# Strassen's seven block products, in fp16, for the output projection of a SwiGLU block behind cosformer attention

## The chip, the cores and the metric

The kernel runs on one core of a Trainium2 chip. The metric is the device time of one execution, in microseconds (us). Most executions of one kernel agree within 0.3%. The kernel before takes 324.7 us (median). Each run also has a profile of one execution: its span (first to last instruction, some 2 us less than the time), the busy time of each engine, and the clock that was granted to TensorE (1.00 is full speed).

The engines have short names in the profile: PE is TensorE (matmuls), PEld its weight loads, DVE VectorE, ACT ScalarE, POOL GpSimd, SP SyncE, which here only issues transfers.

## The reference

```python
# q, k, v: (8, 8, 576, 64) float32.  cosformer attention, then a SwiGLU block
q_p, k_p = phi(q), phi(k)             # relu, times cos and sin of the position
kv  = einsum('bhsf,bhsd->bhfd', k_p, v);  z = k_p.sum(axis=2)
x   = (q_p @ kv) / (q_p . z + 1e-6)   # reshaped to 4608 tokens x 512
g   = x @ w_gate                      # 512 x 1536
out = ((g * sigmoid(g)) * (x @ w_val)) @ w_out      # 1536 x 512
```

## The kernel before

The 4608 tokens are taken in nine groups of 512. For each group TensorE computes gate and value in 12 chunks of 128 hidden columns, with 8 matmuls of 512 columns per chunk. ScalarE makes silu out of PSUM (the memory that matmuls write, here used in eight banks), and VectorE multiplies it with the value into the hidden tile `ht`. Then comes the output projection: four token tiles, each a sum of 12 matmuls of 512 columns in one PSUM bank.

```python
def ffn_mul(tg, fc, lo=0, hi=GH):
    ...
    nc.vector.tensor_tensor(out=hts[tg % 2][:, fc, r:r + n], in0=sg[:, 0:n], in1=ps[1], op=ALU.mult)

def ffn_out(t, f0=0, f1=None):            # one tile of 128 tokens
    ...
    for fc in range(f0, f1):
        nc.tensor.matmul(out=o_ps[t], lhsT=hts[tg % 2][:, fc, r:r + P], rhs=wo_sb[:, fc],
                         start=(fc == 0), stop=(fc == FC - 1))
    ...
    (nc.scalar.copy if t % 2 == 0 else nc.vector.tensor_copy)(out=ob, in_=ps)
    # then two stores of 64 tokens each, on SyncE's queue
```

Work for later groups (the attention of the next batches) is put into numbered slots between these steps: q products (relu on ScalarE, then a multiplication with a table on VectorE), v products, and the normalisation of x. PSUM banks are handed out by a small allocator. It takes the bank that was used longest ago, but for output sums it first looks for a bank whose neighbour is taken, to keep pairs whole for others:

```python
def take(n, hold=None):
    taken = {x for r in held.values() for x in r}
    free = [b for b in range(0, 8, n) if not any(b <= x < b + n for x in taken)]
    b0 = min(free, key=lambda b: (n == 1 and hold is not None and hold[0] == "o" and b ^ 1 not in taken,
                                  sorted(used[b:b + n], reverse=True)))
    ...
```

Of the kernel before, what the change touches and what calls it, by code (L numbers as in the profile page):

```python
# [18 lines left out]
def kernel(  # L19
# [25 lines left out]
    NTG = NH // GH  # L45

# [8 lines left out]
    obp = ctx.enter_context(tc.tile_pool(name="obp", bufs=4))  # L55
# [55 lines left out]
    wo_sb = consts.tile([P, FC, d_model], BF16)  # L111
    hts = [consts.tile([P, FC, T], BF16, name=f"ht_{i}") for i in range(2)]
    first = {"q": consts.tile([P, G, QCUT, D], FP32, name="first_q")}

    for nm, home in (("v", wo_sb), ("k", hts[1])):
        flat = home.rearrange("p a b -> p (a b)")[:, 0:2 * G * NC * D]
        first[nm] = flat.bitcast(FP32).rearrange("p (g c d) -> p g c d", g=G, c=NC)
# [15 lines left out]
    pos_t = consts.tile([P, NW, SH], FP32)  # L133
# [46 lines left out]
    tabq = consts.tile([P, 2, NW, SH], FP16)  # L180
# [162 lines left out]
    qr = [consts.tile([P, 2, J, 2, SH], BF16, name=f"qr_{i}") for i in range(2)]  # L343
    qwT = [consts.tile([P, 2, 2, J, 2, SH], BF16, name=f"qwT_{i}") for i in range(2)]
# [61 lines left out]
    def x_den(t, ps, ys=slice(0, 4)):  # L406
        if ys.start == 0:
            st["den", t] = smp.tile([P, H, 1], FP32, name="den")
        nc.vector.tensor_single_scalar(
            out=st["den", t].rearrange("p (e y) o -> p e y o", e=2)[:, :, ys],  # L410
            in_=ps[:, :, 0:2 * J * D1].rearrange("p e (y x) -> p e y x", x=D1)[:, :, ys, D:D1], scalar=1e-6, op=ALU.add)
# [48 lines left out]
    def x_norm(t):  # L460
        num = st.pop(("num", t)).rearrange("p j e (i x) -> p (j e i) x", i=2)
        den = smp.tile([P, H, 1], FP32, name="den")
        nc.vector.tensor_single_scalar(out=den, in_=num[:, :, D:D1], scalar=1e-6, op=ALU.add)
        rec = smp.tile([P, H, 1], FP32, name="rec")
        nc.vector.reciprocal(out=rec, in_=den)
        x = xp.tile([P, d_model], BF16, name="x")
        for j in range(J):
            hs = slice(4 * j, 4 * j + 4)
            nc.vector.tensor_tensor(
                out=x[:, 4 * j * D:(4 * j + 4) * D].rearrange("p (i e d) -> p e i d", i=2, e=2),  # L470
                in0=num[:, hs, 0:D].rearrange("p (e i) d -> p e i d", e=2),
                in1=rec[:, hs].rearrange("p (e i) o -> p e i o", e=2).to_broadcast([P, 2, 2, D]), op=ALU.mult,
            )
        st["x", t] = x
# [41 lines left out]
    def ffn_silu(tg, fc, lo=0, hi=GH):  # L516
        n = (hi - lo) * SH
        sg = st["s", tg, fc, lo] = sgp.tile([P, T], BF16, name="sg")
        nc.scalar.activation(out=sg[:, 0:n], in_=st["f", tg, fc, lo][0], func=AF.Silu)  # L519

    def ffn_mul(tg, fc, lo=0, hi=GH):
        n, r = (hi - lo) * SH, lo * SH
        ps = st.pop(("f", tg, fc, lo))
        nc.vector.tensor_tensor(out=hts[tg % 2][:, fc, r:r + n], in0=st.pop(("s", tg, fc, lo))[:, 0:n], in1=ps[1],  # L524
# [14 lines left out]
    o_ps = {}  # L539

    def ffn_out(t, f0=0, f1=None):
# [4 lines left out]
        tg, i = divmod(t, GH // 2)  # L546
        r = i * P
        for fc in range(f0, f1):
            nc.tensor.matmul(out=o_ps[t], lhsT=hts[tg % 2][:, fc, r:r + P], rhs=wo_sb[:, fc],  # L549
                             start=(fc == 0), stop=(fc == FC - 1))  # L550
# [4 lines left out]
        ob = obp.tile([P, d_model], FP32, name="ob")  # L555
        (nc.scalar.copy if t % 2 == 0 else nc.vector.tensor_copy)(out=ob, in_=ps)  # L556
        for e in range(2):
            idx = 2 * t + e
            parts = 2 if NH - 10 <= idx < NH - 4 else 1
            for i in range(parts):  # L560
                cols = slice(i * d_model // parts, (i + 1) * d_model // parts)
                nc.sync.dma_start(out=out_v[idx // NC, idx % NC][:, cols], in_=ob[e * SH:(e + 1) * SH, cols])

    def ffn_out_last(t):

        tg, i = divmod(t, GH // 2)
        r = i * P
        for lo, hi in ((0, 320), (320, d_model)):
            ps = take(1)[:, 0:hi - lo]
            for fc in range(FC):  # L570
                nc.tensor.matmul(out=ps, lhsT=hts[tg % 2][:, fc, r:r + P], rhs=wo_sb[:, fc, lo:hi],
                                 start=(fc == 0), stop=(fc == FC - 1))
            ob = obp.tile([P, d_model], FP32, name="ob")
            nc.scalar.copy(out=ob[:, 0:hi - lo], in_=ps)
            for e in range(2):
                idx = 2 * t + e
                (nc.scalar if e else nc.sync).dma_start(out=out_v[idx // NC, idx % NC][:, lo:hi],
                                                        in_=ob[e * SH:(e + 1) * SH, 0:hi - lo])
# [132 lines left out]
    at((0, 1), turn(4), load_2)  # L711
# [69 lines left out]
    for tg in range(1, NTG):  # L781
        s0 = SLOTS * tg
        for fc in range(FC):
            ffn_fc(tg, fc)
            slot(s0 + fc)
        for i in range(OUT):
            if tg == NTG - 1 and i == OUT - 1:
                ffn_out_last(tg * OUT + i)
            else:
                ffn_out(tg * OUT + i)  # L790
            slot(s0 + FC + i)
# [31 lines left out]
```

## Time and profile before

| | kernel before |
|---|---|
| time, median of 4 | 324.67 us |
| span of the profiled execution | 322.9 us |
| TensorE busy | 316.3 us, 98% |
| VectorE busy | 181.0 us, 56% |
| one group's projection, first start to next start | 10.36 us |
| after the last matmul | 4.3 us |

Busy time is an average over stages, so it says who might bound a kernel, not who does. The chain of work that ended last says it: here TensorE has 93% of it. Matmuls overlap in their printed durations, so their cost is read from the distance between starts. The prediction shows these lines. The 4.3 us at the end are an estimate: the last 24 matmuls start at 316.01, and at the 0.109 us of a 256-column matmul (256 is their mean width) they need 2.62 us, which leaves 4.28 up to 322.9.

### The profile page before, as it was taken

To read this page: it belongs to the slowest core of one execution; us is meant where nothing else is said; L and a number is where in the kernel's file an instruction comes from. 1 tells how busy PE (TensorE), PEld (TensorE's weight loads), DVE (VectorE), ACT (ScalarE), POOL (GpSimd) and SP (SyncE) were. 2 spreads that over 40 slices of the span, in tenths; PEclk is the share of its full clock that TensorE was granted. 3 is DMA by queue.
4 is the path that set the end of the run, shared out by engine and by line. 5 is a ranking of instruction groups with operands and counts; after the bars stand their busy time and mean duration, and the time that the engine had idled before them with its cause. 6 is when DMAs were issued, how large, how long until landed. Compare 5 with 4: busy or idle time off the path is not lost.

```text
span 322.9 us, 6033 instructions
## 1 busy us (share of the span) xinstructions
PE 316.3 (98%) x2374; PEld 159.2 (49%) x2384; DVE 181.0 (56%) x363; ACT 130.5 (40%) x239; POOL 35.1 (11%) x60
## 2 busy tenths in 40 slices
PE   8899999999999999999999999999999999999994
PEld 4596555455445444544454445444544444444443
DVE  7873876786448747564756555755573236324320
ACT  7553556652346245333533354335432132213311
POOL 6845002010102000200011000200000000000000
PEclk9999999999999999999999999999999999999999
DMA  7999998988995987699769968895912401240014
GB/s 272 213 200 197 205 195 133 220 106 116 183 192 78 191 150 130 79 177 173 122 92 168 163 119 115 124 194 112 134 34 51 103 11 35 54 92 19 0 26 105
DMA packets 74861, 41.02 MB, mean 127 GB/s; under 512 B 50001, under 2 KB 69969, under 8 KB 74833
## 3 DMA queue, kind: packets, MB, share of 16 engines
q1 hardware_dynamic: 52480, 22.95, 38.9%
q0 software_dynamic: 22192, 17.57, 37.0%
q8 instruction: 18, 0.29, 0.4%
q10 hardware_dynamic: 160, 0.13, 0.1%
q14 instruction: 11, 0.08, 0.1%
HBM read 37.75 MB, written 9.44 MB: 146 GB/s over the span
## 4 chain that ended last, share of the span: by engine, by line
PE 93%; DVE 3%; ACT 2%; DMA 1%; issue 0%; ACTq 0%
PE banks L513 58%; PE banks L549 28%; PE banks L285 3%; PE banks L399 2%; PE banks L444 1%; PE banks L381 1%; DMA out_dram<-ob 1%; DVE v L239 1%; DVE raw_k L220 1%; PE banks L485 0%; DVE qwT L369 0%; ACT L184 0%; ACT phit L333 0%; ACT kvd L297 0%; ACT tabq L181 0%
## 5 line engine op out<-in xcount | busy, mean ns | idle before, releaser
L524 DVE TENSOR_TENSOR ht<-sg,banks 128x512 bf16<-128x512 bf16 (+2 forms) x116 | 74.6, 649 | 68.6 <-PE banks L513 62.1
L513 PE MATMUL banks<-xT,wv_sb 128*128 128x512 bf16 (+2 forms) x464 | 111.3, 364 | 0.0
L513 PE MATMUL banks<-xT,wg_sb 128*128 128x512 bf16 (+2 forms) x464 | 111.3, 364 | 0.0
L519 ACT ACTIVATE sg<-banks 128x512 bf16<-128x512 f32 (+2 forms) x116 | 65.8, 568 | 111.7 <-PE banks L513 109.1
L549 PE MATMUL banks<-wo_sb,ht 128*128 128x512 bf16 x410 | 93.1, 379 | 0.5
L513 PEld LDWEIGHTS <-wv_sb 128*128 128x128 bf16 x464 | 44.8, 98 | 48.7
L513 PEld LDWEIGHTS <-wg_sb 128*128 128x128 bf16 x464 | 43.1, 98 | 42.8
L549 PEld LDWEIGHTS <-ht 128*128 128x128 bf16 x420 | 40.3, 98 | 45.7 <-issue 0.2
L556 ACT COPY ob<-banks 128x512 f32<-128x512 f32 x18 | 10.5, 585 | 54.0 <-PE banks L549 54.0
L235 DVE TENSOR_TENSOR r_q<-raw_q,tab 128x1152 bf16<-128x1152 bf16 x24 | 17.9, 754 | 20.7 <-ACT raw_q L218 20.7
L556 DVE COPY ob<-banks 128x512 f32<-128x512 f32 x17 | 11.7, 691 | 28.7 <-PE banks L549 28.0
L239 DVE TENSOR_TENSOR v<-raw_v,tab 128x1152 bf16<-128x1152 bf16 x31 | 22.7, 752 | 0.3 <-ACT raw_v L583 0.3
L421 DVE TENSOR_TENSOR x<-banks,rec 128x512 bf16<-128x512 f32 (+1 forms) x32 | 21.6, 674 | 1.3 <-PE banks L381 0.3
L218 ACT ACTIVATE raw_k<-raw_k 128x576 bf16<-128x576 bf16 (+1 forms) x25 | 17.0, 694 | 0.0
L218 ACT ACTIVATE raw_q<-raw_q 128x576 bf16<-128x576 bf16 x24 | 15.5, 679 | 0.0
L732 POOL COPY hold<-phit 1x2 bf16<-1x2 bf16 x5 | 0.9, 175 | 130.5 <-DMA phit<-r_q 130.5
L399 PEld LDWEIGHTS <-phit 128*128 128x128 bf16 (+1 forms) x240 | 10.0, 100 | 6.5 <-issue 1.3
L399 PE MATMUL banks<-kv,phit 128*128 128x65 bf16 (+1 forms) x240 | 11.6, 195 | 0.0
L152 PE MATMUL banks<-zeros 128*128 128x64 bf16 (+1 forms) x64 | 9.4, 309 | 1.0 <-DVE zeros L147 1.0
L308 DVE CAST kv<-banks 64x260 bf16<-64x260 f32 x12 | 5.1, 428 | 7.4 <-ACT kv L308 7.3
L285 PEld LDWEIGHTS <-raw_k 64*64 64x64 bf16 x504 | 7.6, 106 | 3.0 <-issue 2.1
L285 PE MATMUL banks<-v,raw_k 64*64 64x130 bf16 x504 | 8.8, 218 | 0.0
(84 smaller groups left out, 130.7 us busy)
## 6 DMA issues: line engine op xcount, KB each, us to landing
out_dram<-ob SPq DMA_DIRECT2D x64, 128.0 KB, 2.4
raw_k<-in_k_dram POOLq DMA_DIRECT2D x7, 576.0 KB, 9.4
raw_q<-in_q_dram POOLq DMA_DIRECT2D x6, 576.0 KB, 6.5
raw_v<-in_v_dram POOLq DMA_DIRECT2D x6, 576.0 KB, 12.7
wo_sb<-in_moe_w_out_dram POOLq DMA_DIRECT2D x3, 512.0 KB, 12.8
wg_sb<-in_moe_w_gate_dram POOLq DMA_DIRECT2D x5, 256.0 KB, 9.2
wv_sb<-in_moe_w_val_dram POOLq DMA_DIRECT2D x5, 256.0 KB, 9.9
wo_sb<-in_v_dram SPq DMA_DIRECT2D x2, 576.0 KB, 4.1
```

The costliest lines, as they stand in the source:

```text
L152: nc.tensor.matmul(out=ps, lhsT=zeros, rhs=zeros[:, 0:cols].unsqueeze(1).to_broadcast([P, 4, cols]), start=True, stop=True)
L218: nc.scalar.activation(out=out, in_=in_, func=AF.Relu)
L235: nc.vector.tensor_tensor(out=st[b, "q"][:, g], in0=o.unsqueeze(2).to_broadcast([P, NC, 2, D]), in1=tab, op=ALU.mult)
L239: nc.vector.tensor_tensor(out=v2s[b % 2][:, g, :, :, 0:D], in0=(first if b == 0 and g == 0 else {"v": raw_of(b, "v")})["v"][:, g].unsqueez ...
L285: nc.tensor.matmul(out=ps[i * D:(i + 1) * D, e, j * 2 * D1:(j + 1) * 2 * D1], lhsT=raws[b, "k"][es, g, c], rhs=v2s[b % 2][es, g, c, :, 0:D ...
L399: nc.tensor.matmul(out=ps[ms, e, g * D1:(g + 1) * D1], lhsT=phit[b][:, e, g, c:c + n].rearrange("p c s -> p (c s)"), rhs=kv2s[b % 2][:, e, ...
L421: nc.vector.tensor_tensor(out=st["x", t].rearrange("p (y e d) -> p e y d", e=2, d=D)[:, :, ys], in0=ps[:, :, 0:2 * J * D1].rearrange("p e ...
L513: nc.tensor.matmul(out=st["f", tg, fc, lo][i], lhsT=(wg_sb, wv_sb)[i][:, kc, fs], rhs=xT[tg][:, ts, kc], start=(kc == 0), stop=(kc == KC - 1))
L519: nc.scalar.activation(out=sg[:, 0:n], in_=st["f", tg, fc, lo][0], func=AF.Silu)
L524: nc.vector.tensor_tensor(out=hts[tg % 2][:, fc, r:r + n], in0=st.pop(("s", tg, fc, lo))[:, 0:n], in1=ps[1], op=ALU.mult)
L549: nc.tensor.matmul(out=o_ps[t], lhsT=hts[tg % 2][:, fc, r:r + P], rhs=wo_sb[:, fc], start=(fc == 0), stop=(fc == FC - 1))
L556: (nc.scalar.copy if t % 2 == 0 else nc.vector.tensor_copy)(out=ob, in_=ps)
```

## The change

Strassen's scheme multiplies two matrices of 2 x 2 blocks with seven block products in place of eight, at the price of additions of blocks. Here the blocks are token halves and halves of the hidden dimension on one side, and hidden and output halves on the other. The intent is to take an eighth off the projection's TensorE time in groups 1 to 8. VectorE makes the sums of hidden blocks (S1 to S4) and adds the products; GpSimd makes the sums of weight blocks (T1 to T4) once. The sums need more mantissa bits, so hidden values and output weights are fp16, with x scaled by 4096 to stay clear of the smallest values. The change also keeps one hidden tile where two alternated.

```diff
-    wo_sb = consts.tile([P, FC, d_model], BF16)
-    hts = [consts.tile([P, FC, T], BF16, name=f"ht_{i}") for i in range(2)]
+    wo_sb = consts.tile([P, FC, d_model], FP16)
+    ht = consts.tile([P, FC, T], FP16, name="ht")
+    wt_sb = consts.tile([P, 4, HC, HD], FP16, name="wt_sb")
...
+    def weight_sums():
+        for o, x, y in ((T1, bq[:, 0, 1], bq[:, 0, 0]), (T2, bq[:, 1, 1], T1), (T3, bq[:, 1, 1], bq[:, 0, 1]),
+                        (T4, bq[:, 1, 0], T2)):
+            nc.gpsimd.tensor_tensor(out=o, in0=x, in1=y, op=ALU.subtract)
...
+    def sums_behind(fc):
+        for n, lo, hi in {7: ((3, 0, 4),), 8: ((1, 0, 4),), 9: ((2, 0, 4),), 10: ((4, 0, 4), (3, 4, 6)),
+                          11: ((1, 4, 6), (2, 4, 6), (4, 4, 6))}.get(fc, ()):
+            token_sum(n, lo, hi)
...
+        a = home("a")
+        product(a, aq[:, 0, 0], bq[:, 0, 0], True)
+        nc.scalar.mul(out=C12, in_=a[0], mul=DOWN)
+        e = home("e")
+        product(e, S3, T3, True)
+        added(C22, e, C12)
+        free("e")
+        slot_of(0)
+        b = home("b", nb)
+        product(b, S2, T2, True)
+        added(C21, b, C22)
+        product(a, aq[:, 1, 0], bq[:, 1, 0], False)
+        nc.scalar.mul(out=C11, in_=a[0], mul=DOWN)
+        free("a")
...
+        product(b, S1, T1, False)
+        added(C22, b, C22)
...
+        c = home("c")
+        product(c, aq[:, 1, 1], T4, True)
+        added(C21, c, C21)
...
+        product(b, S4, bq[:, 1, 1], False)
+        added(C12, b, C12)
...
-    at((0, 1), turn(4), load_2)
+    at((0, 1), turn(4), load_2, weight_sums)
```

A "home" in the code is a PSUM bank. In what follows the "third product" is S2T2, the third in TensorE's order, and the "fifth" is S1T1.

More of the change, by code (lines that the diff above doesn't have):

```diff
@@ L45 @@
     NTG = NH // GH
+    UP = float(2 ** 12)
+    DOWN = 1.0 / UP
+    HC = FC // 2
+    HT = T // 2
+    HD = d_model // 2
     consts = ctx.enter_context(tc.tile_pool(name="consts", bufs=1))
@@ L54 @@
     sgp = ctx.enter_context(tc.tile_pool(name="sgp", bufs=5))
-    obp = ctx.enter_context(tc.tile_pool(name="obp", bufs=4))
+    obp = ctx.enter_context(tc.tile_pool(name="obp", bufs=2))
     psum = ctx.enter_context(tc.tile_pool(name="psum", bufs=1, space=bass.MemoryType.PSUM))
@@ L110, with lodge @@
     CUT = 7
-    wo_sb = consts.tile([P, FC, d_model], BF16)
-    hts = [consts.tile([P, FC, T], BF16, name=f"ht_{i}") for i in range(2)]
-    first = {"q": consts.tile([P, G, QCUT, D], FP32, name="first_q")}
-    for nm, home in (("v", wo_sb), ("k", hts[1])):
+    wo_sb = consts.tile([P, FC, d_model], FP16)
+    ht = consts.tile([P, FC, T], FP16, name="ht")
+    wt_sb = consts.tile([P, 4, HC, HD], FP16, name="wt_sb")
+    spare = wt_sb.rearrange("p a b c -> p (a b c)")
+    taken_up = [0]
+    def lodge(n, dt):
+        o = taken_up[0]
+        taken_up[0] += n * (2 if dt == FP32 else 1)
+        assert taken_up[0] <= 4 * HC * HD
+        part = spare[:, o:taken_up[0]]
+        return part if dt == FP16 else part.bitcast(dt)
+    first = {"q": lodge(G * QCUT * D, FP32).rearrange("p (g c d) -> p g c d", g=G, c=QCUT)}
+    for nm, home in (("v", wo_sb), ("k", ht)):
         flat = home.rearrange("p a b -> p (a b)")[:, 0:2 * G * NC * D]
@@ L132 @@
     nc.gpsimd.iota(pos, pattern=[[1, NC]], base=0, channel_multiplier=NC, allow_small_or_imprecise_dtypes=True)
-    pos_t = consts.tile([P, NW, SH], FP32)
+    pos_t = lodge(NW * SH, FP32).rearrange("p (c s) -> p c s", c=NW)
     nc.gpsimd.iota(pos_t, pattern=[[1, NW], [NC, SH]], base=0, channel_multiplier=0,
@@ L179 @@
     csk, cst = cs_all[:, 0], cs_all[:, 1]
-    tabq = consts.tile([P, 2, NW, SH], FP16)
+    tabq = lodge(2 * NW * SH, FP16).rearrange("p (w c s) -> p w c s", w=2, c=NW)
     nc.scalar.activation(out=tabq[:, 0], in_=pos_t, func=AF.Sin, scale=-rad, bias=half_pi)
@@ L342 @@
     qf = consts.tile([P, 2, J, 2, D], BF16)
-    qr = [consts.tile([P, 2, J, 2, SH], BF16, name=f"qr_{i}") for i in range(2)]
-    qwT = [consts.tile([P, 2, 2, J, 2, SH], BF16, name=f"qwT_{i}") for i in range(2)]
+    qr = [lodge(4 * J * SH, BF16).rearrange("p (e j c s) -> p e j c s", e=2, j=J, c=2) for i in range(2)]
+    qwT = [lodge(8 * J * SH, BF16).rearrange("p (w e j c s) -> p w e j c s", w=2, e=2, j=J, c=2) for i in range(2)]
     def cast_q(c, eng):
@@ L408, in x_den @@
             st["den", t] = smp.tile([P, H, 1], FP32, name="den")
-        nc.vector.tensor_single_scalar(
+        nc.vector.tensor_scalar(
             out=st["den", t].rearrange("p (e y) o -> p e y o", e=2)[:, :, ys],
-            in_=ps[:, :, 0:2 * J * D1].rearrange("p e (y x) -> p e y x", x=D1)[:, :, ys, D:D1], scalar=1e-6, op=ALU.add)
+            in0=ps[:, :, 0:2 * J * D1].rearrange("p e (y x) -> p e y x", x=D1)[:, :, ys, D:D1],
+            scalar1=1e-6, scalar2=DOWN, op0=ALU.add, op1=ALU.mult)
     def x_rec(t, ps, ys=slice(0, 4)):
@@ L462, in x_norm @@
         den = smp.tile([P, H, 1], FP32, name="den")
-        nc.vector.tensor_single_scalar(out=den, in_=num[:, :, D:D1], scalar=1e-6, op=ALU.add)
+        nc.vector.tensor_scalar(out=den, in0=num[:, :, D:D1], scalar1=1e-6, scalar2=DOWN,
+                                op0=ALU.add, op1=ALU.mult)
         rec = smp.tile([P, H, 1], FP32, name="rec")
@@ L518, in ffn_silu @@
         sg = st["s", tg, fc, lo] = sgp.tile([P, T], BF16, name="sg")
-        nc.scalar.activation(out=sg[:, 0:n], in_=st["f", tg, fc, lo][0], func=AF.Silu)
+        nc.scalar.activation(out=sg[:, 0:n], in_=st["f", tg, fc, lo][0], func=AF.Silu, scale=DOWN)
     def ffn_mul(tg, fc, lo=0, hi=GH):
@@ L523, in ffn_mul @@
         ps = st.pop(("f", tg, fc, lo))
-        nc.vector.tensor_tensor(out=hts[tg % 2][:, fc, r:r + n], in0=st.pop(("s", tg, fc, lo))[:, 0:n], in1=ps[1],
+        nc.vector.tensor_tensor(out=ht[:, fc, r:r + n], in0=st.pop(("s", tg, fc, lo))[:, 0:n], in1=ps[1],
                                 op=ALU.mult)
@@ L539, with ob_of, store @@
     o_ps = {}
+    obs = {}
+    def ob_of(t):
+        h, i = divmod(t, 2)
+        if h not in obs:
+            obs[h] = obp.tile([P, 2, d_model], FP32, name="ob")
+        return obs[h][:, i]
+    def store(t, cols=slice(0, d_model), queues=None):
+        for e in range(2):
+            idx = 2 * t + e
+            (queues or (nc.sync, nc.sync))[e].dma_start(out=out_v[idx // NC, idx % NC][:, cols],
+                                                        in_=ob_of(t)[e * SH:(e + 1) * SH, cols])
     def ffn_out(t, f0=0, f1=None):
@@ L545, in ffn_out @@
             o_ps[t] = take(1, ("o", t))
-        tg, i = divmod(t, GH // 2)
-        r = i * P
+        r = t % OUT * P
         for fc in range(f0, f1):
-            nc.tensor.matmul(out=o_ps[t], lhsT=hts[tg % 2][:, fc, r:r + P], rhs=wo_sb[:, fc],
+            nc.tensor.matmul(out=o_ps[t], lhsT=ht[:, fc, r:r + P], rhs=wo_sb[:, fc],
                              start=(fc == 0), stop=(fc == FC - 1))
@@ L554, in ffn_out @@
         give_back(("o", t))
-        ob = obp.tile([P, d_model], FP32, name="ob")
-        (nc.scalar.copy if t % 2 == 0 else nc.vector.tensor_copy)(out=ob, in_=ps)
-        for e in range(2):
-            idx = 2 * t + e
-            parts = 2 if NH - 10 <= idx < NH - 4 else 1
-            for i in range(parts):
-                cols = slice(i * d_model // parts, (i + 1) * d_model // parts)
-                nc.sync.dma_start(out=out_v[idx // NC, idx % NC][:, cols], in_=ob[e * SH:(e + 1) * SH, cols])
@@ L564, in ffn_out_last @@
-    def ffn_out_last(t):
-        tg, i = divmod(t, GH // 2)
-        r = i * P
-        for lo, hi in ((0, 320), (320, d_model)):
-            ps = take(1)[:, 0:hi - lo]
-            for fc in range(FC):
-                nc.tensor.matmul(out=ps, lhsT=hts[tg % 2][:, fc, r:r + P], rhs=wo_sb[:, fc, lo:hi],
-                                 start=(fc == 0), stop=(fc == FC - 1))
-            ob = obp.tile([P, d_model], FP32, name="ob")
-            nc.scalar.copy(out=ob[:, 0:hi - lo], in_=ps)
-            for e in range(2):
-                idx = 2 * t + e
-                (nc.scalar if e else nc.sync).dma_start(out=out_v[idx // NC, idx % NC][:, lo:hi],
-                                                        in_=ob[e * SH:(e + 1) * SH, 0:hi - lo])
+        if t % 2 == 0:
+            nc.scalar.mul(out=ob_of(t), in_=ps, mul=DOWN)
+        else:
+            nc.vector.tensor_single_scalar(out=ob_of(t), in_=ps, scalar=DOWN, op=ALU.mult)
@@ new lines, in ffn_out @@
+        store(t)
+    aq = ht.rearrange("p (i w) (h t) -> p w h i t", w=2, h=2)
+    bq = wo_sb.rearrange("p (i w) (h x) -> p w h i x", w=2, h=2)
+    sums = consts.tile([P, 3, HC, HT], FP16, name="sums")
+    S1, S2, S3, S4 = aq[:, 0, 1], sums[:, 0], sums[:, 1], sums[:, 2]
+    T1, T2, T3, T4 = (wt_sb[:, i] for i in range(4))
+    def weight_sums():
+        for o, x, y in ((T1, bq[:, 0, 1], bq[:, 0, 0]), (T2, bq[:, 1, 1], T1), (T3, bq[:, 1, 1], bq[:, 0, 1]),
+                        (T4, bq[:, 1, 0], T2)):
+            nc.gpsimd.tensor_tensor(out=o, in0=x, in1=y, op=ALU.subtract)
@@ new lines, in token_sum @@
+    def token_sum(n, lo, hi):
+        o, x, y, op = {
+            3: (S3, aq[:, 0, 0], aq[:, 0, 1], ALU.subtract),
+            1: (S1, aq[:, 0, 1], aq[:, 1, 1], ALU.add),
+            2: (S2, S1, aq[:, 0, 0], ALU.subtract),
+            4: (S4, aq[:, 1, 0], S2, ALU.subtract),
+        }[n]
+        nc.vector.tensor_tensor(out=o[:, lo:hi], in0=x[:, lo:hi], in1=y[:, lo:hi], op=op)
+    def sums_behind(fc):
+        for n, lo, hi in {7: ((3, 0, 4),), 8: ((1, 0, 4),), 9: ((2, 0, 4),), 10: ((4, 0, 4), (3, 4, 6)),
+                          11: ((1, 4, 6), (2, 4, 6), (4, 4, 6))}.get(fc, ()):
+            token_sum(n, lo, hi)
@@ new lines, in out_by_quarters, with home, free, at_of @@
+    def out_by_quarters(tg, slot_of):
+        last = tg == NTG - 1
+        t0 = tg * OUT
+        for t in (t0, t0 + 2):
+            ob_of(t)
+        C11, C12 = (obs[t0 // 2][:, :, x * HD:(x + 1) * HD] for x in range(2))
+        C21, C22 = (obs[t0 // 2 + 1][:, :, x * HD:(x + 1) * HD] for x in range(2))
+        def home(nm, parts=1):
+            return [take(1, ("o", tg, nm, i)).rearrange("p (t x) -> p t x", x=HD) for i in range(parts)]
+        def free(nm, parts=1):
+            for i in range(parts):
+                give_back(("o", tg, nm, i))
+        def at_of(x, i):
+            return x[i][:, 0] if len(x) == 2 else x[0][:, i]
+        def product(to, a, b, first):
+            for i in range(2):
+                for kc in range(HC):
+                    nc.tensor.matmul(out=at_of(to, i), lhsT=a[:, kc, i * P:(i + 1) * P], rhs=b[:, kc],
+                                     start=first and kc == 0 and (i == 0 or len(to) == 2),
+                                     stop=kc == HC - 1, skip_group_check=True)
+        def added(o, ps, x):
+            for i in range(len(ps)):
+                sl = slice(i, i + 1) if len(ps) == 2 else slice(0, 2)
+                nc.vector.scalar_tensor_tensor(out=o[:, sl], in0=ps[i][:, 0:1] if len(ps) == 2 else ps[i],
+                                               scalar=DOWN, in1=x[:, sl], op0=ALU.mult, op1=ALU.add)
+        nb = 2 if last else 1
+        a = home("a")
[12 more added lines that the diff above has]
+        free("a")
+        if last:
+            for t in (t0, t0 + 1):
+                store(t, slice(0, HD))
+        slot_of(1)
+        product(b, S1, T1, False)
+        added(C22, b, C22)
+        if last:
+            for t in (t0 + 2, t0 + 3):
+                store(t, slice(HD, d_model))
+        c = home("c")
+        product(c, aq[:, 1, 1], T4, True)
+        added(C21, c, C21)
+        free("c")
+        for t in (t0 + 2, t0 + 3):
+            store(t, slice(0, HD) if last else slice(0, d_model))
+        slot_of(2)
+        product(b, S4, bq[:, 1, 1], False)
+        added(C12, b, C12)
+        free("b", nb)
+        for t in (t0, t0 + 1):
+            store(t, slice(HD, d_model) if last else slice(0, d_model), (nc.sync, nc.scalar) if last else None)
+        slot_of(3)
@@ L784 @@
             ffn_fc(tg, fc)
+            sums_behind(fc)
             slot(s0 + fc)
-        for i in range(OUT):
-            if tg == NTG - 1 and i == OUT - 1:
-                ffn_out_last(tg * OUT + i)
-            else:
-                ffn_out(tg * OUT + i)
-            slot(s0 + FC + i)
+        out_by_quarters(tg, lambda i: slot(s0 + FC + i))
     assert not plan, sorted(plan)
```

## The prediction

> **What bounds the kernel now.** I read the page first: busy shares, then the chain that ended last. Then the chain's lines by shape, then single stretches of the timeline.
>
> ```profile
> PE 316.3 (98%) x2374; PEld 159.2 (49%) x2384; DVE 181.0 (56%) x363; ACT 130.5 (40%) x239; POOL 35.1 (11%) x60
> ...
> PE 93%; DVE 3%; ACT 2%; DMA 1%; issue 0%; ACTq 0%
> PE banks L513 58%; PE banks L549 28%; PE banks L285 3%; PE banks L399 2%; PE banks L444 1%; PE banks L381 1%; DMA out_dram<-ob 1%; DVE v L239 1%; DVE raw_k L220 1%; PE banks L485 0%; DVE qwT L369 0%; ACT L184 0%; ACT phit L333 0%; ACT kvd L297 0%; ACT tabq L181 0%
> ```
>
> TensorE is the bound: 93% of the chain, with the output projection (L549) at 28% of it. TensorE never waits long on another engine, and the granted clock is 1.000. So whatever shortens TensorE's stream shortens the kernel, as long as no other engine starts to hold it up. What a matmul costs must be read from starts, since the printed durations overlap:
>
> ```profile
> 21.27 0.60 PE L513 MATMUL banks<-xT,wg_sb 128*128 128x256 bf16 x4
> 21.71 0.60 PE L513 MATMUL banks<-xT,wv_sb 128*128 128x256 bf16 x4
> 22.14 0.60 PE L513 MATMUL banks<-xT,wg_sb 128*128 128x256 bf16 x4
> 22.58 0.60 PE L513 MATMUL banks<-xT,wv_sb 128*128 128x256 bf16 x4
> 23.02 2.35 PE L513 MATMUL banks<-xT,wg_sb 128*128 128x256 bf16 x20
> 25.20 1.04 PE L513 MATMUL banks<-xT,wv_sb 128*128 128x256 bf16 x8
> ...
> 111.03 10.52 PE L549 MATMUL banks<-wo_sb,ht 128*128 128x512 bf16 x47
> ...
> 121.39 1.03 PE L513 MATMUL banks<-xT,wg_sb 128*128 128x512 bf16 x4
> ```
>
> From 21.27 to 25.20 there are 36 matmuls of 256 columns, each with its own weights: 3.93/36 = 0.109 us. One group's projection is 48 matmuls of 512 columns (47 recorded), from 111.03 to 121.39: 10.36/48 = 0.216 us. A half-width matmul with its own weight load costs half. This is what decides whether Strassen's smaller blocks pay on TensorE at all.
>
> **What the Trainium skill says.** "TensorE: Matmul & The Clock Gate", section "Back-to-back issue gap", gives a warm gap of N/2.4 + 2.5 ns: 109 ns at 256 columns and 216 at 512. The trace agrees to the nanosecond. (The same section's figure of about 131 ns for sustained 512-column matmuls does not fit here.)
>
> "VectorE: DVE Perf Modes", section "What auto-detection actually checks", says that a two-tensor operation reaches two elements a cycle when all tensors are 16-bit with unit step. The trace agrees: L235, 16-bit from SBUF, has 1152 elements in 754 ns, while L421, which reads PSUM, needs 691 ns for 512. The new token sums are of the first kind.
>
> "SBUF — State Buffer", section "Who interferes with whom", says that VectorE and GpSimd share a port pair that one instruction takes for its whole length; a VectorE operation in a two-port mode, or one with two SBUF inputs against a GpSimd instruction that reads SBUF, waits. The first three microseconds show the two-port case:
>
> ```profile
> 1.11 0.59 DVE L170 COPY posk<-pos 64x9 f32<-64x9 f32 x1
> 1.72 0.17 DVE L171 TENSOR_SCALAR posk<-pos 64x9 f32<-64x9 f32 x1
> ...
> 2.12 0.42 DVE L173 TENSOR_SCALAR ang<-posk 128x18 f32<-128x18 f32 x1
> ...
> 0.94 0.59 POOL L134 IOTA pos_t<- 128x512 f32 x1
> ...
> 1.99 0.53 POOL L142 MEMSET kvd<- 128x520 f32 x1
> ```
>
> L170 handles nine elements and takes 0.59 us, ending just after GpSimd's work; L171, of the same size, takes 0.17. L173 ends with the memset. The two-input case is not in this trace.
>
> "GPSIMD Engine Reference", section "Elementwise — side-by-side cycle accounting", gives 4497 ns for a two-input operation of 2048 elements. This trace has no such operation; scaled to 1536 elements my estimate is 3.4 us.
>
> **The change part by part.**
> *TensorE.* Groups 1 to 8 (group 0 keeps the old form) each replace 48 matmuls of 512 columns by 7 products x 2 token halves x 6 = 84 of 256 columns: 84 x 0.109 = 9.18 us for 10.36. That is 1.18 us a group, 9.4 us over eight, all on the chain. It is less than the eighth that the idea promises only through the 2 ns floor per matmul. Fp16 streams as bf16 does, I assume.
>
> *VectorE.* Each group gains four token sums, each cut into 1024 and 512 elements. L235's 754 ns for 1152 elements at 0.52 ns leaves 0.15 us fixed, so they are 0.68 and 0.41 us: 4 x 1.09 = 4.4 us. It gains five additions out of PSUM of 512 elements: L455 takes 483 ns for 260, at 1.04 ns an element, so 0.75 us for 512, together 3.75. It loses two copies of 0.69. Net +6.7 us a group, 54 us over all: 181 becomes 235, 74% of the span. In a middle group (121.4 to 154.9) VectorE has 14.8 + 5.0 = 19.8 us busy and would get 26.5 in about 32.4: no bound on average, but close in places.
>
> *ScalarE.* Two evacuations a group before, two after: nothing.
>
> *Coupling in the output stage.* This is new. One bank collects S2T2, then S1T1 on top, then S4B22 on top, and VectorE must read it before each further product, with one other product (1.31 us) to hide that. I placed a middle group's VectorE work on the old timeline, group 3, with the projection starting at 144.42. The multiplication of chunk 11 ends near 145.2, the three tail sums at 146.5, the pending q product at 147.2, the normalisation of the next x (1.04) at 148.25, the addition of S3T3 at 148.9, a q product at 149.6, the addition of S2T2 at 150.3. TensorE wants the bank at 144.42 + 4 x 1.31 = 149.66, so it waits about 0.65 us. The next reuse (at 152.9 against a read done at 152.5) fits. Groups 1 to 5 have q products in this place, in group 1 with later sums; groups 6 to 8 do not, and there the read ends in time. I book 5 x 0.6 = 3.0 us.
>
> *Weight sums on GpSimd.* Four two-input operations, 4 x 3.4 = 13.6 us, once, queued behind the loads of batch 2. They must be there for group 1's projection near 78 us, which is easy. But they start at about 51.05, when group 0's last x is made:
>
> ```profile
> 50.30 0.75 POOL L102 DMA_DIRECT2D raw_v<-in_v_dram  x1
> ...
> 51.67 0.17 DVE L463 TENSOR_SCALAR den<-num 128x8 f32<-128x8 f32 x1
> 51.87 0.20 DVE L465 RECIPROCAL rec<-den 128x8 f32<-128x8 f32 x1
> ...
> 52.11 0.76 DVE L469 TENSOR_TENSOR x<-num,rec 128x256 bf16<-128x256 f32 x2
> ...
> 53.00 0.39 PE L485 MATMUL banks<-ident,x 128*128 128x128 bf16 x4
> ```
>
> L463 is SBUF to SBUF like L173, L469 has two SBUF inputs, and TensorE transposes the result at 53.00 with 0.1 us to spare. If the first weight sum holds the ports until 54.45, x comes at about 55.65 and TensorE loses 2.7 us. If the second gets in between L463 and L469, it comes at about 58.9 and TensorE loses 5.9, and might fall to a lower clock after such a pause. If the lock does not bite, nothing. I book 2.0 us as a mean.
>
> *Ends.* The start only moves where small tables lie. At the end a 256-column addition on VectorE (about 0.48 us) takes the place of a 192-column copy (0.32) before the last stores: +0.2 us.
>
> Sum: 324.7 - 9.4 + 3.0 + 2.0 + 0.2 = 320.5.
>
> **The rivals.**
> *The full gain.* VectorE is earlier than I think, and GpSimd disturbs nothing: 324.7 - 9.4 = 315.3. For it: TensorE's share of the chain, and the half-width rate, which is measured. Against it: the dense VectorE queue.
> *VectorE paces every output stage.* If the sums run at one element a cycle, they cost about 3.3 us a group more; chunks 7 to 11 take TensorE some 9.2 us, and VectorE would be late for S2 and for each bank read, by 1.5 to 2.5 us a group: 324 to 330. Against it: L235's rate on like operands.
> *GpSimd's sums cost most of the gain.* Three blocked operations in a row, 6 to 10 us and a lower clock after it: 324 to 330. For it: L170 and L173. Against it: it happens only once, and later VectorE work has some 4 us of slack behind TensorE's eight banks.
> *Weight loads no longer hide.* A load is 98 ns busy, and a 256-column matmul leaves 109. Were they to add, the change would lose tens of microseconds; the 36 matmuls above exclude it.
>
> **Range and chances.** The 9.4 us are firm to half a microsecond. The output stalls can be 0.5 to 6 us, the GpSimd block 0 to 6, rarely 10. Both small gives 316; both large 326. Faster by over 2% means below 318.2, which needs the two together under 2.9 us: 0.30. Slower than 331.2 needs a rival in full: 0.05. The rest, 0.65, is within 2%.
>
> **What would show it.** The 256-column matmuls should start 0.109 us apart, and an undisturbed output stage should last 9.2 us; if they start farther apart without any wait, the first step is wrong. TensorE should wait for VectorE's additions once in each of groups 1 to 5, 0.4 to 0.8 us, and hardly in 6 to 8. The token sums should take 0.68 and 0.41 us; about 1.2 and 0.7 would show one element a cycle. The weight sums should take 3 to 4 us each, and between 51 and 59 us the lines that were L463 and L469 should be stretched, with TensorE idle before the transposes; if they are not, the port step is wrong. A granted clock under 1.0 after 53 us would be the part that I did not price.

## The result

The changed kernel takes 347.27 us (345.22 to 349.61 in four runs) beside 324.67 before. The ratio is 1.0699, with a 95% interval of 1.0642 to 1.0756. Here and below a ratio is the mean time of one kernel's fast runs over that of the other's of the same rounds, so it isn't quite the ratio of the medians. The outputs are correct. This is 7% slower, where I predicted 1.3% faster.

The page of the changed kernel, first its busy times, then the clock granted to TensorE in 40 equal slices (tenths), then the chain that ended last:

```profile
PE 310.9 (91%) x2660; PEld 186.5 (54%) x2660; DVE 236.6 (69%) x455; ACT 130.2 (38%) x237; POOL 47.9 (14%) x64
...
PEclk9999997699999999999999999999999999999997
...
PE 65%; DVE 13%; DMA 10%; SPq 4%; issue 3%; ACT 2%; DVEq 0%; POOLq 0%; POOL 0%; ACTq 0%
```

TensorE's busy time fell by 5 us and its share of the chain from 93 to 65%: it waits now, mostly for VectorE. VectorE has 236.6 us, where I had predicted 235. In two slices, 51 to 69 us, the clock fell (in the last slice TensorE has almost nothing to do). Most of the chain's 10% of DMA lies in groups 3 and 4: there the chain is followed back from an addition on VectorE over a q product to the transfers that brought its operand. TensorE ran without gaps during these transfers, so they are not lost time.

Where the 20.4 us between the spans came from is told by the starts of the stages on TensorE in both timelines:

| stage | before | after | difference |
|---|---|---|---|
| to the first matmul of group 1 | 54.09 | 63.60 | +9.51 |
| chunks of group 1 | 23.32 | 24.45 | +1.13 |
| projections of groups 1 to 5 | 51.8 | 57.6 | +5.8 |
| projections of groups 6 to 8 | 31.1 | 30.7 | -0.4 |
| after the last matmul | 4.3 | 8.6 | +4.3 |
| all other stages | | | 0.0 |

The chunk stages of groups 2 to 8 are among these, so the single hidden tile cost nothing there.

Three places, then. The first is the end of group 0's projection. GpSimd's, VectorE's and TensorE's timelines of the changed kernel (start, duration, engine, line, operation, output and input):

```profile
51.88 3.10 POOL L602 TENSOR_TENSOR wt_sb<-wo_sb 128x1536 f16<-128x1536 f16 x1
55.06 3.08 POOL L602 TENSOR_TENSOR wt_sb<-wo_sb,wt_sb 128x1536 f16<-128x1536 f16 x1
58.10 3.26 POOL L602 TENSOR_TENSOR wt_sb<-wo_sb 128x1536 f16<-128x1536 f16 x1
...
51.56 3.46 DVE L480 TENSOR_SCALAR den<-num 128x8 f32<-128x8 f32 x1
55.05 0.20 DVE L483 RECIPROCAL rec<-den 128x8 f32<-128x8 f32 x1
55.29 6.35 DVE L487 TENSOR_TENSOR x<-num,rec 128x256 bf16<-128x256 f32 x2
...
58.48 0.40 PE L503 MATMUL banks<-ident,x 128*128 128x128 bf16 x2 [5.43 <-DVE x L487]
61.70 0.40 PE L503 MATMUL banks<-ident,x 128*128 128x128 bf16 x2 [2.83 <-DVE x L487]
...
63.60 1.91 PE L531 MATMUL banks<-xT,wg_sb 128*128 128x512 bf16 x4
```

The den operation (the denominator of x), 0.17 us before, took 3.46 and ended with the first weight sum. Each of the two halves of x then ended with the second and the third: 6.35 us for 0.76. TensorE stood for 8.3 us, and then ran at half clock: the four matmuls at 63.60 are 1.91 us long, where those before were 1.03.

The second place is each projection. Group 2 of the changed kernel, where the bracket gives the idle time before an instruction and what ended it, and the same product of group 8:

```profile
122.51 1.47 PE L640 MATMUL banks<-wo_sb,ht 128*128 128x256 f16 x12
123.82 1.47 PE L640 MATMUL banks<-wt_sb,sums 128*128 128x256 f16 x12
127.55 1.47 PE L640 MATMUL banks<-wt_sb,sums 128*128 128x256 f16 x12 [2.26 <-DVE ob L647]
128.86 1.47 PE L640 MATMUL banks<-wo_sb,ht 128*128 128x256 f16 x12
...
126.82 0.68 DVE L647 SCALAR_TENSOR_TENSOR ob<-banks,ob 128x512 f32<-128x512 f32 x1
...
328.15 1.47 PE L640 MATMUL banks<-wt_sb,sums 128*128 128x256 f16 x12 [0.84 <-DVE ob L647]
```

A product is 12 matmuls, and products start 1.31 us apart: 0.109 us each, as predicted. But the third product does not follow the second. It waits for the addition of S3T3 on VectorE, in all eight groups, even in group 8, where VectorE stood idle before it. Start to start beyond 1.31 us, the eight waits are 1.84, 2.42, 2.40, 1.95, 2.23, 1.00, 1.21 and 1.00: 14.05 us. Less the 9.4 us that seven products save, that leaves +4.65; the two rows of the table give +5.4, and the rest is smaller waits, above all 0.2 us before the seventh product in groups 1 to 5.

Why should S2T2 wait for the reading of S3T3? The two need no common data. I wrote the allocator's answers down while building the kernel: for group 3 it gives bank 2 to `a`, 3 to `e`, and 3 again to `b`. (A second build with the answers printed confirms this, and shows the bank of `e` again in `b` in all eight groups.) The program gives `e` back just before it asks for `b`, and the neighbour of `a`, which is the bank of `e`, is what the allocator looks for first.

The third place is the end, from SyncE's and ScalarE's queues:

```profile
333.38 1.47 PE L640 MATMUL banks<-wo_sb,sums 128*128 128x256 f16 x12
...
331.59 9.36 SPq L570 DMA_DIRECT2D out_dram<-ob  x14
334.74 1.38 ACTq L570 DMA_DIRECT2D out_dram<-ob  x2
```

Sixteen stores fall due within the last three or four microseconds, and 14 of them are issued one after another on one queue: 9.36/14 = 0.67 us each. The kernel before had twelve on that queue, and two on ScalarE's, spread over the projection of the last group.

### The profile page after: what moved, and what is told of

It is laid out like the page before. It is cut to its first block, busy times and chain, and to the rows that moved or that the text cites. A ratio compares the mean times of both kernels' runs of the same rounds, so it can differ in the third digit from the quotient of the medians.

```text
span 343.3 us, 6710 instructions
## 1 busy us (share of the span) xinstructions
PE 310.9 (91%) x2660; PEld 186.5 (54%) x2660; DVE 236.6 (69%) x455; ACT 130.2 (38%) x237; POOL 47.9 (14%) x64
## 4 chain that ended last, share of the span: by engine, by line
PE 65%; DVE 13%; DMA 10%; SPq 4%; issue 3%; ACT 2%; DVEq 0%; POOLq 0%; POOL 0%; ACTq 0%
PE banks L531 40%; PE banks L640 18%; DMA phit<-r_q 5%; DMA raw_q<-in_q_dram 4%; DVE x L487 2%; SPq L570 2%; SPq L274 2%; DVE ob L647 2%; PE banks L301 2%; DVE ht L542 2%; DVE sums L611 2%; PE banks L580 2%; DVE den L480 1%; PE banks L415 1%; DVE r_q L251 1%
## 5 line engine op out<-in xcount | busy, mean ns | idle before, releaser
L542 DVE TENSOR_TENSOR ht<-sg,banks 128x512 f16<-128x512 bf16 (+2 forms) x116 | 74.6, 648 | 53.0 <-PE banks L531 44.6
L647 DVE SCALAR_TENSOR_TENSOR ob<-banks,ob 128x512 f32<-128x512 f32 (+1 forms) x43 | 28.0, 652 | 19.5 <-PE banks L640 18.5
L640 PEld LDWEIGHTS <-ht 128*128 128x128 f16 x384 | 37.1, 98 | 4.5
L640 PEld LDWEIGHTS <-sums 128*128 128x128 f16 x288 | 28.1, 98 | 18.3 <-issue 15.2
L640 PE MATMUL banks<-wt_sb,sums 128*128 128x256 f16 x192 | 23.6, 272 | 12.7 <-DVE ob L647 12.7
L640 PE MATMUL banks<-wo_sb,ht 128*128 128x256 f16 x192 | 23.6, 273 | 0.0
L640 PE MATMUL banks<-wt_sb,ht 128*128 128x256 f16 x192 | 22.3, 273 | 0.0
L663 ACT ACTIVATE ob<-banks 128x512 f32<-128x512 f32 x8 | 4.8, 597 | 36.4 <-PE banks L640 36.4
L611 DVE TENSOR_TENSOR sums<-ht 128x1024 f16<-128x1024 f16 (+1 forms) x32 | 17.7, 553 | 0.3
L580 PE MATMUL banks<-wo_sb,ht 128*128 128x512 f16 x48 | 13.0, 400 | 0.0
```

Source lines behind the costliest of these rows:

```text
L542: nc.vector.tensor_tensor(out=ht[:, fc, r:r + n], in0=st.pop(("s", tg, fc, lo))[:, 0:n], in1=ps[1], op=ALU.mult)
L580: nc.tensor.matmul(out=o_ps[t], lhsT=ht[:, fc, r:r + P], rhs=wo_sb[:, fc], start=(fc == 0), stop=(fc == FC - 1))
L611: nc.vector.tensor_tensor(out=o[:, lo:hi], in0=x[:, lo:hi], in1=y[:, lo:hi], op=op)
L640: nc.tensor.matmul(out=at_of(to, i), lhsT=a[:, kc, i * P:(i + 1) * P], rhs=b[:, kc], start=first and kc == 0 and (i == 0 or len(to) == 2), ...
L647: nc.vector.scalar_tensor_tensor(out=o[:, sl], in0=ps[i][:, 0:1] if len(ps) == 2 else ps[i], scalar=DOWN, in1=x[:, sl], op0=ALU.mult, op1= ...
```

## The experiments

Nine kernels ran, all correct. The changed kernel's time is 347.27 us.

My theory is that the three places are three separate faults: GpSimd's hold on the ports, a bank shared by two products, and a queue of stores. The rivals are given with each run.

### Weight sums on VectorE

```diff
-            nc.gpsimd.tensor_tensor(out=o, in0=x, in1=y, op=ALU.subtract)
+    def weight_sums(ns=(0, 1, 2, 3), eng=nc.vector):
...
+            eng.tensor_tensor(out=o, in0=x, in1=y, op=ALU.subtract)
-    at((0, 1), turn(4), load_2, weight_sums)
+    at((0, 1), turn(4), load_2)
+    at(SLOTS + 2, lambda: weight_sums((0, 1)))
+    at(SLOTS + 3, lambda: weight_sums((2, 3)))
```

> The four weight sums move from GpSimd in group 0's projection to VectorE in group 1 (two at chunk 2, two at chunk 3, about 0.95 us each); all else as changed. Theory: the GpSimd sums held VectorE's den and x operations and cost TensorE about 9.5 us of waiting and 1.1 us of lower clock, so this is 10 to 11 us faster than the changed kernel (about 335 us), TensorE's wait before the last transposes of group 0 is under 0.3 us, the granted clock is 1.00, and the runs no longer scatter between 345 and 349. Rival: TensorE would have waited there anyhow, for the transfers or for x itself; then it gains under 3 us. A second rival: VectorE pays in group 1 what it gains; then TensorE waits over 2 us in group 1.

Measured: 337.75 us (335.28 to 338.94), 9.5 us under the changed kernel, a little less than the 10 to 11 expected. Group 1 starts at 54.03 in place of 63.60. A sum takes 0.95 us on VectorE. In group 1 TensorE waits for VectorE for about 1.1 us in all, so the second rival, over 2 us, fails. So the sums on GpSimd were the cause of the first loss. The scatter did not go, against what I expected: granted clocks are 0.984 to 0.993, and in this trace the clock falls to 0.50 after the third product of group 2 has waited 2.26 us. It does not fall after a wait of 2.30 us in the next group.

### The same sums on GpSimd, meant to be later

```diff
-    at((0, 1), turn(4), load_2, weight_sums)
-    at((2, 2), turn(7, True))
+    at((0, 1), turn(4), load_2)
+    at((2, 2), turn(7, True), weight_sums)
```

> The weight sums stay on GpSimd but are queued after the last transposes of group 0, some 2 us later in program order. Theory (it is the place that costs, since x is needed at once there, while group 1's VectorE work has about 4 us of slack): the wait before the transposes goes, VectorE's q products and v products of group 1 are stretched to about 3 us instead, and the time is 7 to 11 us under the changed kernel. Rival (13 us of GpSimd sums cost TensorE the same wherever they lie): within 2 us of the changed kernel, with TensorE's waits in group 1 instead.

Measured: 345.64 us (344.75 to 348.83), the same as the changed kernel. The trace shows why this is no answer: the first sum starts at 51.91 us, as before. Nothing on GpSimd's queue waits for the transposes, so a later place in the program is not a later time. The experiment was badly made, and the next one mends it.

### The sums on GpSimd, held back until x has been used

```diff
-    at((0, 1), turn(4), load_2, weight_sums)
-    at((2, 2), turn(7, True))
+    at((0, 1), turn(4), load_2)
+    at((2, 2), turn(7, True), lambda: nc.gpsimd.tensor_copy(out=hold2, in_=xT[1][0:1, 3, 0, 0:2]), weight_sums)
```

> The changed kernel with one more GpSimd copy ahead of the weight sums, which reads the last transposed x of group 0's projection, so that the sums really start after it (at about 53.5 us and not 51.9). Theory (the place costs, because x is wanted at once): TensorE's pause of 8 us before the transposes goes; VectorE's q products, v products and den of group 1 are held for up to 3 us each instead, and the time falls by 5 to 10 us. Rival (13 us of GpSimd sums cost the same wherever VectorE has two-input operations): TensorE's pauses reappear inside group 1, and the time falls by under 3 us.

Measured: 344.67 us (343.65 to 346.05), 2.6 us under the changed kernel and not clear of the scatter of both. The sums start at 54.37 now, and the transposes of group 0 do not wait. From VectorE's and TensorE's timelines of this run:

```profile
56.68 4.96 DVE L251 TENSOR_TENSOR r_q<-raw_q,tab 128x1152 bf16<-128x1152 bf16 x2
...
62.16 6.60 DVE L251 TENSOR_TENSOR r_q<-raw_q,tab 128x1152 bf16<-128x1152 bf16 x2
...
69.41 1.86 PE L531 MATMUL banks<-xT,wv_sb 128*128 128x512 bf16 x4 [5.45 <-DVE ht L542]
```

Two pairs of q products, 1.42 us each pair in the other kernels, took 4.96 and 6.60. The multiplications into `ht` stood behind them in VectorE's order, TensorE ran out of free banks, waited 5.45 us, and came back at a lower clock. My theory that only the place was bad falls; the rival holds. I had written in the prediction that VectorE's work there has some 4 us of slack; 8.7 us of extra holding is more than that.

### Writes in place of the sums

The weight sums are on VectorE as in the first experiment, and GpSimd writes zeros where its sums were (two executions in place of four):

```diff
+    at((0, 1), turn(4), load_2,
+       lambda: [nc.gpsimd.memset(sums..., 0.0) for _ in range(5)])
```

> Weight sums on VectorE; in their old place GpSimd writes zeros into the token-sum tile five times, about 2.4 us each, reading nothing. It tells which VectorE operations are held by what. Theory from the skill: den (one SBUF source, two-port mode) is held by a GpSimd write, up to 2.5 us or to the end of the run of writes; x (two SBUF inputs) is held only by a GpSimd operation that reads, so its two operations stay at 0.76 us together. Rival: any GpSimd operation holds both; then x takes 2 us or more as well.

Measured: 337.54 us (336.32 and 338.77), against 337.75 in the first experiment. GpSimd's and VectorE's timelines:

```profile
51.44 10.35 POOL L821 MEMSET sums<- 128x2304 f32 x5
...
51.42 2.10 DVE L480 TENSOR_SCALAR den<-num 128x8 f32<-128x8 f32 x1
...
53.79 0.76 DVE L487 TENSOR_TENSOR x<-num,rec 128x256 bf16<-128x256 f32 x2
...
58.20 1.42 DVE L251 TENSOR_TENSOR r_q<-raw_q,tab 128x1152 bf16<-128x1152 bf16 x2
```

This is the distinction of the Trainium skill's page "SBUF — State Buffer", section "Who interferes with whom", seen on one trace. Den, with one source in SBUF (the memory in which the tiles lie), is held by a GpSimd write: 2.10 us for 0.17. Operations with two SBUF inputs are not: x takes 0.76 and the q products 1.42, although the writes run until 61.8. Against GpSimd sums, which read, the same two took 6.35 and 4.96. The writes are not quite free: behind the late den TensorE waits 1.36 us in this trace, and group 1 starts at 55.59 for 54.03. So the larger part of the loss, 5.6 of the 8.9 us for which VectorE was held, comes from GpSimd instructions that read SBUF beside VectorE instructions with two SBUF inputs, and not from GpSimd being busy; the 3.3 us of den are of a kind that a write causes too.

### A bank of its own for the third product

```diff
         added(C22, e, C12)
-        free("e")
         slot_of(0)
         b = home("b", nb)
+        free("e")
```

> The third product S2T2 gets a PSUM bank of its own: it is taken before the bank of S3T3 is given back. Nothing else changes. Theory: the 14 us of waits before the third product (0.84 to 2.3 us in each of the eight groups) come from sharing that bank with S3T3, which VectorE has yet to read; they vanish, and the waits that I had predicted before the fifth product take their place in groups 1 to 5, about 0.6 to 1.1 us each. So 8 to 12 us faster than the changed kernel. Rival: the third product waits for the token sums of S2, which come late on VectorE; then the waits stay and the time changes by under 2 us.

Measured: 334.05 us (333.86 to 334.45), 13.2 us under the changed kernel by one line that moved two lines down. From the lists of waits, first of the changed kernel, then of this one (total, times, longest):

```profile
PE banks L640 <- DVE ob L647: 12.7, 8, 2.3
```

```profile
PE banks L640 <- DVE ob L647: 2.8, 5, 0.9
```

Eight waits before the third product are gone. Five are left, all before the fifth product, in groups 1 to 5: 0.33, 0.91, 0.56, 0.30 and 0.71 us. That is the wait that I had predicted, at 3.0 us in all; in the changed kernel another one stood in its place. (The later answers of the allocator change with the moved line: the sixth product no longer gets the bank of `a`. No wait is listed before it in either run.) The runs also lie within 0.6 us of each other, while all kernels with the shared bank scatter by 2.4 us or more. Between the two profiled executions the gain is 11.1 us (span 343.3 to 332.2), where start to start the waits fell from 14.05 to 3.6 us and the 0.2 us before each seventh product went too, so the waits account for it. The larger gain of the medians is not explained by waits: in the changed kernel's two slower executions the clock is 0.969 in place of 0.976 and 0.979, which fits drops of the clock behind the longer waits, but there is no trace of those two.

### Stores on two queues

```diff
-            (queues or (nc.sync, nc.sync))[e].dma_start(...)
+            (queues or ((nc.sync, nc.scalar) if t >= OUT * (NTG - 1) else (nc.sync, nc.sync)))[e].dma_start(...)
```

> Only the last group's stores change: half of them go to ScalarE's queue, where all but two went to SyncE's. Theory: the last 8.6 us after the last matmul are the issue of 14 stores one after another at about 0.6 us each on one queue; with two queues the end comes 3.5 to 4.5 us sooner. Rival: the stores are bound by the DMA engines or the landing of the last one; then under 1 us.

Measured: 344.16 us (341.00 to 345.28). The scatter of the shared bank covers the size, so the trace decides: the last matmul ends at 338.02 (start of the last product plus 1.31) and the span at 343.2, which is 5.2 us, where the changed kernel had 8.6. The gain is 3.4 us, just under the range expected. This run also shows a clock drop at its worst. In the projection of group 2 the third product came after a wait of 3.39 us, and in that stretch the mean granted clock was 0.74:

```profile
122.00:135.00 13.00, 9.61 (x66) 7.17 (x65) 6.65 (x15) 2.93 (x6) 0.00 (x0) 0.74 0.98 162
```

(The columns are the stretch, its length, the busy time of PE, PEld, DVE, ACT and POOL, then the clock, the DMA share and GB/s.)

### All three together

> The three single edits together: weight sums on VectorE, a bank of its own for S2T2, the last group's stores on two queues. Theory: the three losses are separate and add up: about 10.6 + 11 + 3.4 us under the changed kernel's undisturbed span of 343.3, that is 318 to 320 us, and with no long pause left the granted clock stays at 0.99 or more and the runs lie within 1 us. Rival: something common lies behind them (VectorE as a whole is too slow), and one loss grows when another is removed; then over 325 us.

The edits are the three of above. Measured: 321.58 us (320.60 to 322.46), ratio to the kernel before 0.9908 (0.9884 to 0.9932), span 319.7. The three losses do add up, within 2 us: the changed kernel is turned from 7% slower to 0.9% faster, which is clear of noise. The clock is 0.996 or more in all runs. The median lies 1.6 us above what I expected, and the runs scatter by 1.9 us, not 1. In the trace TensorE waits 2.7 us before fifth products and about 1.1 us in group 1, where VectorE now makes the weight sums.

### Rearranged

```diff
+    at((2, 3), lambda: weight_sums((0, 1)))
+    at(SLOTS + 2, lambda: weight_sums((2,)))
+    at(SLOTS + 3, lambda: weight_sums((3,)))
...
         added(C22, e, C12)
-        free("e")
-        slot_of(0)
         b = home("b", nb)
+        free("e")
         product(b, S2, T2, True)
         added(C21, b, C22)
+        slot_of(0)
```

The stores are on two queues as well.

> An attempt to beat the kernel before: as the three edits together, but the four weight sums lie apart on VectorE (two after group 0's last copy, one each at chunks 2 and 3 of group 1), and the q product that stood between the additions of S3T3 and S2T2 comes after both. Theory: the waits before the fifth product in groups 1 to 5 (2.8 us in all with the own bank) shrink under 0.5 us, and group 1 does not wait for VectorE; so 315.5 to 318 us, 2 to 3% under the kernel before. Rival: the q product moved back meets the next addition and the wait moves to the seventh product; then 318 to 320 us.

Measured: 318.29 us (317.77 to 319.13), ratio 0.9816 (0.9797 to 0.9835). This beats both kernels, but the interval lies across 0.98, so "faster by 2%" is unclear, and the median is just above the 315.5 to 318 expected. Its page:

```profile
PE 308.4 (98%) x2660; PEld 186.4 (59%) x2660; DVE 230.6 (73%) x459; ACT 130.3 (41%) x237; POOL 35.2 (11%) x60
...
PEclk9999999999999999999999999999999999999998
```

TensorE is at 98% again, with 7.9 us less to do than in the kernel before. One wait before a fifth product is left, 0.44 us in group 2, and no wait moved to the seventh product. Projections last 9.36 us in groups 3 to 5, for 10.36 before. Two edits came together here, and what each is worth was not tested.

### Stores on three queues

```diff
-                store(t, slice(HD, d_model))
+                store(t, slice(HD, d_model), (nc.gpsimd, nc.gpsimd))
```

> As the rearranged kernel, but four of the last group's sixteen stores (the lower right quarter, ready first but one) go to GpSimd's queue, so that the other two queues have six each and are empty when the last sums are ready. Theory: the end is still bound by issue, eight stores at about 0.69 us on each queue; the time after the last matmul falls from 5.1 to about 4.4 us, so 0.5 to 0.9 us off: 317.4 to 317.8. Rival: the end is bound by the landing of the last store (2.1 us) or GpSimd's queue is slower; then no gain, or a loss of up to 1 us.

Measured: 318.42 us (317.99 to 319.54), ratio 0.9812: the same. After the last matmul there are 5.1 us, as with two queues. Six stores were issued between 308.61 and 313.71 us on SyncE's queue, but one by one an issue takes 0.54 us at the median; the queue also stood waiting for VectorE:

```profile
SPq L570 <- DVE ob L648: 1.4, 1, 1.4
```

The theory that the number of stores on each queue still bounds the end falls: a queue with fewer stores waits for the data of the last ones. The last addition ends at 312.34, two more issues on ScalarE's queue last until 314.03, and a store lands 2.0 to 3.2 us after its issue. That accounts for the end by the trace, but no run was made to shorten any of these.

## Why the prediction was wrong

By its own steps:

**Matmul rate and gross gain: right.** The 256-column matmuls start 0.109 us apart, fp16 streams as bf16 did, and group 8's projection without its wait is 9.16 us for a predicted 9.18. The 9.4 us are there; the rearranged kernel has 6.2 us of them in its time.

**VectorE's work: right by the piece, the total by luck.** Token sums take 0.68 and 0.42 us for 0.68 and 0.41, additions 0.69 for 0.75. That the whole is 236.6 us for 235 is luck: it counts 8.9 us in which den and x were only held. With the sums on VectorE the page shows 230.9, and without the 3.8 us of these sums 227, so I had put the work about 8 us too high. The rival "VectorE paces every output stage" at one element a cycle did not come true.

**"Coupling in the output stage": wrong wait, and mis-sized.** The step that failed is "One bank collects S2T2, then S1T1 on top, then S4B22 on top", because it takes the bank to be that product's own from the start. In the program it is the bank of S3T3 first. TensorE therefore waited before the third product, with no other product to hide the addition, in all eight groups: 14.05 us in place of the 3.0 that I booked, and a group without other VectorE work still lost 1.0 us. With the banks apart, the waits that I had worked out appear: five of them, 2.8 us in all (3.6 from start to start). I had the allocator's rule in front of me and never applied it to the seven products.

**"Weight sums on GpSimd": right mechanism, wrong size.** The lock did what the rival described: den waited for the first sum, and each half of x for a further one. A sum takes 3.1 to 3.3 us for an estimated 3.4. I booked 2.0 us "as a mean", and the place cost 10.6: 9.5 up to the first matmul of group 1, and 1.1 by the half clock after it. The start of this trace had already shown an operation held to the end of GpSimd's work. A mean between nothing and six was the wrong way to book it; the arguments for the lock were measured, and those against it were not. The argument against, "it happens only once, and later VectorE work has some 4 us of slack", is disproved twice: once is enough where x is wanted at once, and in group 1 the sums cost nearly the same (344.67 us for 347.27).

**"Ends": wrong.** I booked +0.2 us for the longer addition and did not count the stores. Sixteen of them fall due together where 14 came spread out, and the end grew by 4.3 us.

**The range.** I let the two uncertain terms be small or large together and stopped at 326; by my own upper ends, 6 us each, the sum is 327.5. Both came out above their upper ends, and a third was missing: 2.0 + 3.0 + 0.2 booked, 10.6 + 14.9 + 4.3 in fact (14.9 is the +5.4 of the projections and the 9.4 gained). That is 24.6 us more, and with the profiled execution's 345.22 us it is the whole miss. Drops of the clock fit the 4 us of scatter between executions, but this is not shown.

## What to carry to other kernels

Work out for every new product which physical buffer it gets, by the allocator's own rule and order of freeing, before looking for the waits: one line moved here was worth 11 us between the profiled executions and 13 between the medians. An elementwise GpSimd operation that reads SBUF is not free beside a busy VectorE, since each VectorE operation with two SBUF inputs can wait for a whole GpSimd instruction; 3.8 us of work on VectorE replaced 13 us on GpSimd. When a stage is reordered, count the stores that fall due at its end and the queue that issues them.

## What the Trainium skill lacked or had wrong

- "SBUF — State Buffer", section "Who interferes with whom": the rule agrees with all runs here, write-only case included. It lacks what happens with a chain of dependent operations: between two of them the next GpSimd instruction takes the ports, so each link waits for a whole one. Den took 3.46 us for 0.17, and two halves of x 6.35 for 0.76, behind sums of 3.1 us each.
- "TensorE: Matmul & The Clock Gate", section "Why this matters for your kernels": it advises against idle gaps over about 3 us. In these runs shorter waits could do it: in the run with the sums held back, the clock fell to half after waits of 2.26 and 2.06 us, and stayed at full speed after 2.38 us in the same execution.
- The same page, section "Back-to-back issue gap": the figure of 131 ns for sustained 512-column matmuls does not fit; 216 ns before, and 109 ns at 256 columns, agree with its formula for a single gap.
- "GPSIMD Engine Reference", section "Elementwise — side-by-side cycle accounting": it has no fp16 figure. Its 4497 ns for 2048 elements in fp32 scales to an estimate of 3.4 us for 1536; in fp16 the sums took 3.1 to 3.3 us in the changed kernel and up to 3.6 where they were held back.
- "DMA: Bandwidth & Descriptors", section "Issuing engines are not separate DMA queues": it says that issuing from several engines only saves issue time, "usually small relative to the DMA itself". Here 14 stores issued one after another on SyncE's queue took 0.67 us each, beside 2.1 us from issue to landing, and spreading them gave 3.4 us at the end of the kernel. The section has no figure for one issue.
